# First block of a sliding-window attention: far scores preset in PSUM, two value products ahead, output weights split later, second norm's rows loaded sooner, the inverse roots of two tiles computed together

## The chip, the cores and the metric

The kernel runs on one core of a Trainium2 chip. The metric is the device time of one execution in microseconds; the median of three runs of the kernel before is 2051.01 (2048.93 to 2053.45).

## What is computed

Two layers of the same pair of blocks act on x, 2048 rows of 640 numbers. Each block normalizes its rows first and adds its result to x.

```
def _A_ref(x, dft_seq_re, dft_seq_im, dft_hid_re, dft_hid_im):
    a = jnp.einsum("bsd,ed->bse", x, dft_hid_re)
    b = jnp.einsum("bsd,ed->bse", x, dft_hid_im)
    y = jnp.einsum("ts,bse->bte", dft_seq_re, a) - jnp.einsum("ts,bse->bte", dft_seq_im, b)
    return y
...
    H = 32; Dh = D // H; W = 256
    ...
    scores = jnp.einsum("bhqd,bhkd->bhqk", q, k) * (Dh ** -0.5)
    idx = jnp.arange(S)
    mask = (idx[:, None] - idx[None, :] >= 0) & (idx[:, None] - idx[None, :] < W)
    scores = jnp.where(mask[None, None], scores, -1e9)
    p = _softmax(scores, axis=-1)
    o = jnp.einsum("bhqk,bhkd->bhqd", p, v)
    return (lambda x, *d: x.transpose(*d))(o, 0, 2, 1, 3).reshape(B, S, D) @ wo
...
x = x + _A_ref(_layernorm(x, axis=-1), ...)
x = x + _B_ref(_layernorm(x, axis=-1), B_wqkv, B_wo)
x = x + _A_ref(_layernorm(x, axis=-1), ...)
x = x + _B_ref(_layernorm(x, axis=-1), B_wqkv, B_wo)
```

The layer norm is (x - mean) / sqrt(variance + 1e-5), without weights. A query sees its own key and the 255 before it.

## The kernel before

The program is four stages, one after the other: `spectral(0)`, `attention(0)`, `spectral(1)`, `attention(1)`. In the profiled execution attention 0 runs from about 553 to 1062 us and attention 1 from about 1565 to 2052 us.

**Steps of an attention.** The 2048 rows are 16 tiles of 128 (index `i`), two of which make a block of 256 rows (`b`, 0 to 7). The main loop counts steps `G`; a block has 16 of them, and each step takes two of the 16 pairs of heads of one tile. In the code `g` is 2 G and `r` its place in a block of 32. One step issues, in this order:

- `scores`: TensorE computes the scores of this step's heads against the tile two back ("far", a = 0) into the front of the PSUM tiles `sk` (called `farq`), and against the tile before and its own tile (a = 1, 2) into the PSUM tiles `sq` (`near`). There is one `sq` and one `sk` for each of two partition groups `pi`, and no second buffer: the scores of the next step wait until this step's are read.
- `by_key`: the transposed scores of the step 8 before, into the rest of `sk`.
- `largest`, once for each `pi`: VectorE copies by a mask (L1175, COPY_PREDICATED) those far scores that a query sees into `near`, over those of its own tile that it doesn't see, and takes the largest of each query (L1177, TENSOR_REDUCE into `m`). In the first block (`i` < 2, steps 0 to 15) no far tile exists; then the copy reads `neg`, a 128 x 128 tile in SBUF filled with -1e20, broadcast over the two heads.
- after odd steps `part_tops` on GpSimd (POOL), `hand_on` of the maxima, `probabilities` (a sigmoid on ScalarE, L1231, and one or two affine selects on POOL, L1235 and L1237), `values` of step G - 11, and `back` (RECIPROCAL `r` and TENSOR_TENSOR `o` on VectorE, L1279 and L1280, then POOL's two ops on `os`).
- one *unit* of 15 matmuls (`run_unit`): a part of the projections to queries and keys (`proj_qk`), to values (`proj_v`), of the output product (`out_tile`, whose sum with x on VectorE is L956), or of the next stage.
- `slow_step`: one `yield` of the slow work in the queues `slow` and `idle`. It may not be issued ahead of the step's last reduction (`tc.issue_after(topped[0])`). How often it is called is in `STEPS`: once in even steps, twice in odd ones, and once more in the first steps (g below 14).

**Slow work.** `rows_norm` normalizes two tiles of x for the block after next: `norm_steps` (statistics on VectorE, an inverse square root by three Newton steps, L148 to L152, and the scaled rows `lny`, L166), then `split` into two fp16 parts, for which POOL does a subtraction into `rx` (L178). In the root, every op works on one column of 128 numbers, for the two tiles one after the other: two ops, then three times L151 and L152. Its x rows (`x2`) are loaded by SP's DMA queue some steps ahead, at most one pair at a time. `split_wo` splits the output weights into fp16 parts `bo` (ScalarE L1013, VectorE L1014); in layer 0 it is put into `idle` ahead of the main loop. `next_norm` does one tile's norm for the next spectral stage.

**Ahead of the loop**, `run_fill(FIRST_FILL)` issues units of the first value product until 2000 ns are spent: one of 15 matmuls (15 x 136 ns).

`marks` and `in_line` keep the order of instructions on one engine as written: an instruction issued within `in_line("dve")` is placed no sooner than the last one marked "dve". Otherwise the tile scheduler places the instructions of each engine.

Of the kernel before, what the change touches and what calls it, by code (L numbers as in the profile page):

```python
# [11 lines left out]
F32 = mybir.dt.float32  # L12
# [22 lines left out]
THIN_TO = (240, 264)  # L35
FIRST_FILL = 2000
FILL_LAST = 8
# [8 lines left out]
BACK_LAG = 12  # L46
STEPS = ((1, 2), (1, 2))
MUST_TO = 20
# [24 lines left out]
def body(ctx: ExitStack, tc: tile.TileContext, x_in, cmat, whid, wqkv, wo, out):  # L73
# [14 lines left out]
    mask = pers.tile([P, P], I32, name="mask")  # L88
    neg = pers.tile([P, P], F32, name="neg")
    shift = pers.tile([P, 1], F32, name="shift")  # L90
# [3 lines left out]
    def constants():  # L94
        make_identity(nc, idf[:])
        nc.vector.tensor_copy(idh, idf)
        nc.gpsimd.memset(mask, 1)
        nc.gpsimd.memset(neg, NEG)
        nc.gpsimd.memset(shift, SHIFT)
        for k in range(2):  # L100
            nc.gpsimd.memset(ones[:, k], M_UP if k else 0.0)
            nc.sync.dma_start(ones_d[k].rearrange("a (b c) -> (a b) c", c=2 * NP * QB // P), ones[:, k])
        nc.gpsimd.affine_select(out=mask, in_=mask, pattern=[[1, P]], base=0, channel_multiplier=-1,
                                compare_op=OP.is_gt, fill=0.0)
# [27 lines left out]
    def norm_steps(xs, ys, act=False):  # L132
# [12 lines left out]
        ts = nc.vector.tensor_scalar  # L145
        for k in range(n):
            h, g, u = (t[:, m, k:k + 1] for m in range(3))
            ts(h, mv[:, k, 1:2], 1e-5, -0.5 * X_UP ** -2, op0=OP.add, op1=OP.mult)  # L148
            ts(g.bitcast(I32), h.bitcast(I32), -0.5, ROOT, op0=OP.mult, op1=OP.add)
            for m in range(3):  # L150
                ts(u, g, g, h, op0=OP.mult, op1=OP.mult)  # L151
                normed[0] = ts(g, u, 1.5, g, op0=OP.add, op1=OP.mult).ins  # L152
                if m == 0:
                    yield
            if act:
                normed[0] = ts(u, mv[:, k, 0:1], g, -1.0, op0=OP.mult, op1=OP.mult).ins
            yield
# [688 lines left out]
    def attention(layer, proj, dst, final):  # L846
        with ExitStack() as st:
# [11 lines left out]
            farq = [t[:, :2 * P].rearrange("p (e c) -> p e c", e=2) for t in kst]  # L859
            tps = [t[:, 2 * P:].rearrange("p (a e c) -> p e a c", a=3, e=2) for t in kst]  # L860
            in_turn[0] = True
            VS_ = {}
# [80 lines left out]
            def out_tile(i):  # L943
                ot = OT[i]
                x3 = x2 = X2.pop(i)
                for n in range(2):
# [3 lines left out]
                    for dt in range(ND):  # L950
                        for l, r in ((0, 0), (0, 1), (1, 0)):
                            matmul(pf[:, :320], ot[:, l, dt], bo[r][:, dt, cs], start=k == 0, stop=k == 14)
                            k += 1
                            if k < 15:
                                yield 136
                    nc.vector.scalar_tensor_tensor(x3[:, cs], pf[:, :320], beta, x2[:, cs], op0=OP.mult, op1=OP.add)  # L956
                    yield 136
# [210 lines left out]
            def largest(G, pi):  # L1168
                i, p0 = place(2 * G)
                n, k = divmod(G, 2)  # L1170
                if k == 0 and pi == 0:
                    TOP[n] = sb.tile([P, 2, 2, 2], F32, tag="m", name="m", bufs=3)
                far = farq[pi] if i >= 2 else neg[:, None, :].to_broadcast([P, 2, P])
                with in_line("dve"):
                    marks["dve"] = nc.vector.copy_predicated(near[pi][:, :, 0], mask[:, None, :].to_broadcast([P, 2, P]), far).ins  # L1175
                with in_line("dve"):
                    marks["dve"] = nc.vector.tensor_reduce(TOP[n][:, pi, :, k], near[pi][:, :, :1 + (i >= 1)], axis=AX.XY, op=OP.max).ins  # L1177
                topped[0] = marks["dve"]
# [138 lines left out]
            def slow_step():  # L1317
                with tc.issue_after(topped[0]), in_line("act"):
                    for line in (slow, idle):
# [9 lines left out]
            spent[0] = credit[0] = 0.0  # L1329
            if layer == 0:  # L1330
                idle.append(split_wo())
            def due(G, lag):
                n, m = divmod(G - lag, 2)
                return n if m == 0 and 0 <= n < NG // 4 else None

            wanted, x2s, normed_at = [], [], [-FREE_STEPS]
            turned_back = []
            for G in range(NS // 2 + 1):
# [36 lines left out]
                if g < NG and c < NBQ and (g == 0 or r == X2_STEP):  # L1375
                    wanted.append(c)
                if wanted and x2s and g >= x2s[0] + 4 * (g > 0):
                    slow.append(rows_norm(wanted.pop(0), x2s.pop()))
                    x2s.clear()
                if slow:  # L1380
                    normed_at[0] = g
                if wanted and not slow and not x2s and g >= normed_at[0] + FREE_STEPS:
                    x2s += [g, [keep.tile([P, D], F32, tag="res0", name="x2", bufs=2) for t in range(2)]]
                    for t in range(2):
                        load(x2s[1][t], x2_d[2 * wanted[0] + t])
                if g < NG and r == ROWS_STEP:
                    flush(("v", b))
# [4 lines left out]
                if g < NG and r == HIDDEN_STEP:  # L1392
                    if b == NBQ - 1 and not final:
# [3 lines left out]
                        for k in range(2):  # L1397
                            fill.append(Unit(g + NEXT_STEPS[k], hidden.stage(k, None, once=True), "next", NG + k))
                for _ in range(STEPS[layer][G % 2] + (g < ROWS_STEP)):
                    slow_step()  # L1400
# [18 lines left out]
                if ran and turned_back:  # L1419
                    with in_line("dve"):  # L1420
                        back(turned_back.pop())
            while unit[0] is not None or fill or slow or idle or later:
                now[0] += 1
# [38 lines left out]
```

## Time and profile before

| | us |
|---|---|
| median of three runs | 2051.01 |
| profiled execution | 2055.41 |
| its span | 2053.7 |
| around the span | 1.7 |
| TensorE (PE) busy | 1986.1 |
| VectorE (DVE) busy | 1568.6 |
| GpSimd (POOL) busy | 1475.1 |
| ScalarE (ACT) busy | 1112.4 |

The profile is one execution; its times are microseconds from the span's start. A row of the timeline gives start, duration, engine, line and operation, the tile written and those read, and in brackets the idle time of the engine before it with what ended it. `xN` is a count of instructions. `pf<-big,early` is a product of values or of the output, `pf<-early,big` of queries and keys. The row of a window gives its length, then the busy time of PE, of its weight loads, of DVE, ACT and POOL, and then the granted clock of TensorE as a share of the full one.

### The profile page before, as it was taken

How to read it: one execution, taken by the hardware profiler on the slowest of the kernel's cores; microseconds unless marked ns; L12 is line 12 of the kernel's file. 1: busy time of each engine (PE TensorE's matmuls, PEld its weight loads, DVE VectorE, ACT ScalarE, POOL GpSimd, SP SyncE). 2: the span in 40 equal slices, each digit the busy share in tenths (PEclk: the TensorE clock that was granted, in tenths of full speed). 3: DMA queues.
4: the chain of work that ended last, by engine and by line, in shares of the span. 5: the costliest groups of instructions: out<-in, count | busy, mean ns of one | idle time of the engine just before them, and what ended most of it. 6: DMA issues, size and time to landing. Idle time of an engine off the chain costs nothing.

```text
span 2053.7 us, 55762 instructions
## 1 busy us (share of the span) xinstructions
PE 1986.1 (97%) x21881; PEld 1449.5 (71%) x21881; DVE 1568.6 (76%) x3261; ACT 1112.4 (54%) x1959; POOL 1475.1 (72%) x2168
## 2 busy tenths in 40 slices
PE   6999999999989999999999999999999999999998
PEld 4777777776767777777667777777676677777765
DVE  8888778768588888777648778787776788886673
ACT  5544555534247777666644444444332576766665
POOL 5777788877457788776657778777783587777754
PEclk9999999999999999999999999999999999999999
DMA  7556566566544544434645455454744454443232
GB/s 274 178 197 203 174 209 226 179 242 215 148 111 102 126 125 112 105 93 103 166 132 177 153 184 178 151 172 145 284 161 129 88 129 118 120 121 95 72 85 74
DMA packets 280508, 311.10 MB, mean 151 GB/s; under 512 B 107572, under 2 KB 214836, under 8 KB 271156
## 3 DMA queue, kind: packets, MB, share of 16 engines
q1 hardware_dynamic: 279668, 306.88, 50.0%
q8 instruction: 171, 2.80, 0.6%
q14 instruction: 93, 0.76, 0.1%
q10 hardware_dynamic: 576, 0.66, 0.1%
HBM read 201.72 MB, written 83.46 MB: 139 GB/s over the span
## 4 chain that ended last, share of the span: by engine, by line
PE 69%; DVE 14%; issue 5%; POOL 4%; DMA 4%; ACT 3%; SPq 0%; DVEq 0%; POOLq 0%; ACTq 0%
PE pf L126 32%; PE y L126 11%; PE x L126 11%; PE z L126 7%; PE sk L126 5%; DVE cc L558 3%; PE sq L126 3%; DVE sq L1175 2%; DVE m L1177 2%; ACT ptq L1231 2%; DMA res<-accd 2%; DVE lnt L151 1%; POOL cs L548 1%; DVE res L581 1%; DVE lnst L139 1%
## 5 line engine op out<-in xcount | busy, mean ns | idle before, releaser
L126 PEld LDWEIGHTS <-cc 128*128 128x128 f16 x5376 | 524.4, 98 | 213.1 <-issue 13.4
L1231 ACT ACTIVATE ptq<-sk,shift,alpha 128x768 f32<-128x768 f32 (+2 forms) x512 | 472.5, 945 | 122.9 <-PE sk L126 70.7
L126 PEld LDWEIGHTS <-big 128*128 128x128 f16 x4320 | 415.1, 99 | 131.0 <-issue 25.0
L1177 DVE TENSOR_REDUCE m<-sq 128x2 f32<-128x512 f32 (+1 forms) x512 | 345.6, 675 | 19.4 <-POOL os L1282 0.5
L126 PE MATMUL pf<-early,big 128*128 128x256 f16 x2400 | 295.1, 277 | 0.1
L555 ACT ACTIVATE cc<-cs 128x512 f16<-128x512 f32 x256 | 153.7, 625 | 260.3 <-POOL cs L548 149.8
L126 PE MATMUL y<-zc,cc 128*128 128x320 f16 x1728 | 262.8, 299 | 3.2 <-DVE pf L581 3.2
L1235 POOL TENSOR_SCALAR_AFFINE_SELECT ptq<-ptq 128x512 f32<-128x512 f32 x224 | 142.7, 637 | 167.7 <-ACT ptq L1231 165.1
L558 DVE SCALAR_TENSOR_TENSOR cc<-cs,cc 128x512 f16<-128x512 f32 x256 | 248.1, 978 | 7.6 <-ACT cc L555 7.5
L1175 DVE COPY_PREDICATED sq<-mask,sk 128x256 f32<-128x256 int32 x448 | 189.5, 423 | 53.4 <-PE sq L126 51.6
L558 DVE SCALAR_TENSOR_TENSOR cc<-cq,cc 128x512 f16<-128x512 f32 x192 | 205.8, 1073 | 0.1
L126 PE MATMUL pf<-ptq,v 128*32 128x128 f32 (+1 forms) x3840 | 183.6, 329 | 3.1 <-DVE x L956 2.6
L126 PE MATMUL z<-zc,cc 128*128 128x320 f16 x1152 | 177.7, 299 | 5.4 <-DVE res L581 4.4
L1237 POOL TENSOR_SCALAR_AFFINE_SELECT ptq<-ptq 128x512 f32<-128x512 f32 x256 | 166.1, 649 | 19.6 <-ACT ptq L1231 19.4
L126 PE MATMUL x<-zc,cc 128*128 128x320 f16 x1152 | 177.7, 299 | 0.0
L387 ACT ACTIVATE qf<-pf 128x256 f32<-128x256 f32 x160 | 61.2, 383 | 166.1 <-PE pf L126 132.8
L126 PEld LDWEIGHTS pf<-ptq,v 128*32 128x32 f32 x3840 | 110.7, 110 | 45.5 <-DVE x L956 3.9
L126 PE MATMUL pf<-big,early 128*128 128x320 f16 x960 | 141.4, 300 | 0.0
L547 POOL TENSOR_TENSOR cs<-cq 128x512 f32<-128x512 f32 x64 | 86.8, 1357 | 68.3 <-DVE cc L558 67.7
L126 PEld LDWEIGHTS <-qs 62*128 62x128 f16 x2688 | 90.3, 94 | 59.1 <-issue 55.8
L126 PE MATMUL pf<-bo,ot 128*128 128x320 f16 x840 | 123.8, 300 | 0.8 <-DVE x L956 0.8
L126 PE MATMUL x<-big 128*128 128x320 f16 x825 | 122.3, 299 | 2.0 <-DVE big L447 2.0
(144 smaller groups left out, 3484.3 us busy)
## 6 DMA issues: line engine op xcount, KB each, us to landing
cq<-in_cmat_dram SPq DMA_DIRECT2D x64, 1024.0 KB
accd<-res SPq DMA_DIRECT2D x96, 320.0 KB
res<-accd SPq DMA_DIRECT2D x96, 320.0 KB
x<-x2d SPq DMA_DIRECT2D x64, 320.0 KB
qkd<-early SPq DMA_DIRECT2D x160, 128.0 KB
ks<-qkd SPq DMA_DIRECT2D x108, 160.0 KB
qs<-qkd SPq DMA_DIRECT2D x84, 160.0 KB
x2d<-res SPq DMA_DIRECT2D x32, 320.0 KB
```

The costliest lines, as they stand in the source:

```text
L126: i = getattr(nc.tensor, what)(*args, **kw)
L139: nc.vector.bn_stats(st[:, h], x[:, h * 320:(h + 1) * 320])
L151: ts(u, g, g, h, op0=OP.mult, op1=OP.mult)
L387: nc.scalar.activation(f, pf[:, :QB], AF.Copy, scale=down)
L547: g.tensor_tensor(s1, a21, a22, op=OP.add)
L555: nc.scalar.activation(cc[m][:, 0], f, AF.Copy, scale=C_UP)
L558: nc.vector.scalar_tensor_tensor(cc[m][:, 1], f, C_UP, cc[m][:, 0], op0=OP.mult, op1=OP.subtract)
L1175: marks["dve"] = nc.vector.copy_predicated(near[pi][:, :, 0], mask[:, None, :].to_broadcast([P, 2, P]), far).ins
L1177: marks["dve"] = nc.vector.tensor_reduce(TOP[n][:, pi, :, k], near[pi][:, :, :1 + (i >= 1)], axis=AX.XY, op=OP.max).ins
L1231: marks["act"] = nc.scalar.activation(o[:, pi], tps[pi][:, :, first:], AF.Sigmoid, bias=shift, scale=alpha[:, 0:1]).ins
L1235: nc.gpsimd.affine_select(out=q[:, :, a0], in_=q[:, :, a0], pattern=[[0, 4], [-1, P]], base=0, channel_multiplier=1, compare_op=OP.is_gt, ...
L1237: ins = nc.gpsimd.affine_select(out=q[:, :, a0 + 2], in_=q[:, :, a0 + 2], pattern=[[0, 4], [1, P]], base=0, channel_multiplier=-1, compare ...
```

## The change

1. `FIRST_FILL` is 4000: two units of the first value product are issued ahead of the loop.
2. The front of both `sk` tiles is set to -1e20 by VectorE at the start of each attention, and the masked copy reads it there in the first block too. `neg` and POOL's memset of it are gone.
3. `split_wo` goes into `idle` at g = 14 and not ahead of the loop.
4. The times at which a pair's rows are loaded and its norm may begin are set otherwise: a load may be issued as soon as the norm before has ended, and the norm itself keeps the distance.
5. `norm_steps` for more than one tile works on both columns at once: two TENSOR_SCALAR, then three times two TENSOR_TENSOR and a SCALAR_TENSOR_TENSOR.
6. In even steps the slow steps are issued behind the unit, and slow work is placed no sooner than the last sum of an output tile (`marks["x"]`).

```
-FIRST_FILL = 2000
+FIRST_FILL = 4000
...
-STEPS = ((1, 2), (1, 2))
+STEPS = (1, 2)
...
-        for k in range(n):
+        if n > 1 and not act:
+            h, g, u = (t[:, m] for m in range(3))
+            ts(h, mv[:, :, 1], 1e-5, -0.5 * X_UP ** -2, op0=OP.add, op1=OP.mult)
+            ts(g.bitcast(I32), h.bitcast(I32), -0.5, ROOT, op0=OP.mult, op1=OP.add)
+            for m in range(3):
+                nc.vector.tensor_tensor(u, g, g, op=OP.mult)
+                nc.vector.tensor_tensor(u, u, h, op=OP.mult)
+                normed[0] = nc.vector.scalar_tensor_tensor(g, u, 1.5, g, op0=OP.add, op1=OP.mult).ins
+                yield
+        for k in range(n if n == 1 or act else 0):
...
+            for f in farq:
+                nc.vector.memset(f, NEG)
...
-                    nc.vector.scalar_tensor_tensor(x3[:, cs], pf[:, :320], beta, x2[:, cs], op0=OP.mult, op1=OP.add)
+                    marks["x"] = nc.vector.scalar_tensor_tensor(x3[:, cs], pf[:, :320], beta, x2[:, cs], op0=OP.mult, op1=OP.add).ins
...
-                far = farq[pi] if i >= 2 else neg[:, None, :].to_broadcast([P, 2, P])
...
-                    marks["dve"] = nc.vector.copy_predicated(near[pi][:, :, 0], mask[:, None, :].to_broadcast([P, 2, P]), far).ins
+                    marks["dve"] = nc.vector.copy_predicated(near[pi][:, :, 0], mask[:, None, :].to_broadcast([P, 2, P]), farq[pi]).ins
...
-                with tc.issue_after(topped[0]), in_line("act"):
+                with tc.issue_after(topped[0]), in_line("act"), in_line("x"):
...
-            if layer == 0:
-                idle.append(split_wo())
...
-            wanted, x2s, normed_at = [], [], [-FREE_STEPS]
+            wanted, x2s, normed_at = [], [], [-2 * FREE_STEPS]
...
-                if wanted and x2s and g >= x2s[0] + 4 * (g > 0):
+                if wanted and x2s and g >= max(x2s[0] + 4 * (g > 0), normed_at[0] + 2 * FREE_STEPS):
...
-                if wanted and not slow and not x2s and g >= normed_at[0] + FREE_STEPS:
+                if wanted and not slow and not x2s and g > normed_at[0]:
...
+                if layer == 0 and g == ROWS_STEP:
+                    idle.append(split_wo())
...
-                for _ in range(STEPS[layer][G % 2] + (g < ROWS_STEP)):
+                steps = STEPS[G % 2] + (g < ROWS_STEP)
+                for _ in range(steps if G % 2 else 0):
...
+                for _ in range(0 if G % 2 else steps):
+                    slow_step()
```

What stands on VectorE shows it best. These rows are VectorE's order before, in the first block of attention 0, from the second reduction of step 0 to the second copy of step 2 (`sq` of one number is group 0, of the other group 1):

```order
L1177 TENSOR_REDUCE m<-sq_6969 128x2
L1175 COPY_PREDICATED sq_6968<-mask,neg 128x256
L1177 TENSOR_REDUCE m<-sq_6968 128x2
L1175 COPY_PREDICATED sq_6969<-mask,neg 128x256
L1177 TENSOR_REDUCE m<-sq_6969 128x2
L1014 SCALAR_TENSOR_TENSOR bo_67<-wst,wsc,bo_66 128x640
L1175 COPY_PREDICATED sq_6968<-mask,neg 128x256
L1014 SCALAR_TENSOR_TENSOR bo_67<-wst,wsc,bo_66 128x640
L1177 TENSOR_REDUCE m<-sq_6968 128x2
L1175 COPY_PREDICATED sq_6969<-mask,neg 128x256
```

And these are the same place in the changed kernel, whose line numbers are some higher (the masked copy is L1183, the reduction L1185), from the two new memsets on:

```order
L869 MEMSET sk_6963 128x256
L869 MEMSET sk_6964 128x256
L1183 COPY_PREDICATED sq_6961<-mask,sk_6963 128x256
L1185 TENSOR_REDUCE m<-sq_6961 128x2
L1183 COPY_PREDICATED sq_6962<-mask,sk_6964 128x256
L1185 TENSOR_REDUCE m<-sq_6962 128x2
L1183 COPY_PREDICATED sq_6961<-mask,sk_6963 128x256
L1185 TENSOR_REDUCE m<-sq_6961 128x2
L1183 COPY_PREDICATED sq_6962<-mask,sk_6964 128x256
L1185 TENSOR_REDUCE m<-sq_6962 128x2
```

The two ops on `bo` have left this place (they stand behind the reductions of step 11 now), and every copy reads `sk` in place of `neg`.

The second place is the root of a pair in a later block, as it stands in VectorE's order before, from the last reduction of step 43 to the first copy of step 44:

```order
L1177 TENSOR_REDUCE m<-sq_6969 128x2
L148 TENSOR_SCALAR lnt<-lnmv 128x1
L149 TENSOR_SCALAR lnt<-lnt 128x1
L151 TENSOR_SCALAR lnt<-lnt 128x1
L152 TENSOR_SCALAR lnt<-lnt 128x1
L151 TENSOR_SCALAR lnt<-lnt 128x1
L152 TENSOR_SCALAR lnt<-lnt 128x1
L151 TENSOR_SCALAR lnt<-lnt 128x1
L1279 RECIPROCAL r<-pf 128x8
L152 TENSOR_SCALAR lnt<-lnt 128x1
L1280 TENSOR_TENSOR o<-pf,r 128x160
L1175 COPY_PREDICATED sq_6968<-mask,sk_6970 128x256
```

The changed kernel has there:

```order
L1185 TENSOR_REDUCE m<-sq_6962 128x2
L146 TENSOR_SCALAR lnt<-lnmv 128x2
L147 TENSOR_SCALAR lnt<-lnt 128x2
L149 TENSOR_TENSOR lnt<-lnt 128x2
L150 TENSOR_TENSOR lnt<-lnt 128x2
L151 SCALAR_TENSOR_TENSOR lnt<-lnt 128x2
L149 TENSOR_TENSOR lnt<-lnt 128x2
L150 TENSOR_TENSOR lnt<-lnt 128x2
L151 SCALAR_TENSOR_TENSOR lnt<-lnt 128x2
L1287 RECIPROCAL r<-pf 128x8
L1288 TENSOR_TENSOR o<-pf,r 128x160
L1183 COPY_PREDICATED sq_6961<-mask,sk_6963 128x256
```

Eight ops of one column, which are all of the first tile's root, became eight of two columns, which are two thirds of both tiles' roots; both `r` and `o` stand behind them. The rest of the root and the second tile's, four steps of slow work before, shrink to three ops behind the reductions of step 44.

On TensorE the matmuls are the same; a unit of the value product (15 x `pf<-big,early`) stands ahead of the first scores of each attention now, and the units of the following steps move up. The transposes of the first norms in `spectral(0)` stand two matmuls later.

More of the change, by code (lines that the diff above doesn't have):

```diff
@@ L88, in body @@
     mask = pers.tile([P, P], I32, name="mask")
-    neg = pers.tile([P, P], F32, name="neg")
     shift = pers.tile([P, 1], F32, name="shift")
@@ L97, in constants @@
         nc.gpsimd.memset(mask, 1)
-        nc.gpsimd.memset(neg, NEG)
         nc.gpsimd.memset(shift, SHIFT)
```

## The prediction

> **What bounds the kernel now.** I read the page first (busy shares), then the windows around the first block of each attention, then PE's waits there and its timeline, and last VectorE (DVE) and GpSimd (POOL) side by side.
>
> ```profile
> span 2053.7 us, 55762 instructions
> PE 1986.1 (97%) x21881; PEld 1449.5 (71%) x21881; DVE 1568.6 (76%) x3261; ACT 1112.4 (54%) x1959; POOL 1475.1 (72%) x2168
> ```
>
> TensorE is the bound: only 2053.7 - 1986.1 = 67.6 us of the span are without a matmul. A change that leaves the matmuls as they are can win only from those gaps and from stretches where the matmuls run at a lower clock. The windows show both; PEclk is the granted TensorE clock, and PE's busy time stands right behind the length of the window.
>
> ```profile
> 575.00:590.00 15.00, 12.47 (x106) 9.56 (x106) 10.74 (x25) 4.42 (x11) 9.61 (x18) 0.89 0.46 101
> 590.00:625.00 35.00, 32.82 (x381) 22.45 (x381) 30.21 (x76) 20.08 (x43) 20.59 (x45) 0.95 0.46 101
> ...
> 1585.00:1600.00 15.00, 12.47 (x96) 9.12 (x95) 9.49 (x19) 4.35 (x10) 10.00 (x18) 0.77 0.51 116
> 1600.00:1632.00 32.00, 29.65 (x346) 20.33 (x344) 26.25 (x69) 17.11 (x37) 17.05 (x38) 0.95 0.45 90
> ```
>
> In these four windows, the first blocks of the two attentions, PE idles 2.53, 2.18, 2.53 and 2.35 us, and the missing clock is 15 x 0.11 = 1.65, 35 x 0.05 = 1.75, 15 x 0.23 = 3.45 and 32 x 0.05 = 1.60 us. Together 9.6 us of idling and 8.45 us of clock. PE's waits say what ends the idling. The first two rows are the window 556 to 575, the next is 575 to 700, then 1585 to 1700, and the last one 700 to 960.
>
> ```profile
> PE sq L126 <- DMA x2d<-res: 2.1, 1, 2.1
> PE sq L126 <- DVE m L1177: 2.0, 3, 1.2
> ...
> PE sq L126 <- DVE m L1177: 5.0, 7, 1.5
> ...
> PE sq L126 <- DVE m L1177: 4.7, 6, 1.5
> ...
> PE pf L126 <- DVE x L956: 2.1, 5, 0.8
> ```
>
> PE's timeline shows the places (start, duration, in brackets the idle time before):
>
> ```profile
> 557.44 0.27 PE L126 MATMUL sq<-ks 62*128 62x128 f16 x3 [2.11 <-DMA x2d<-res]
> 557.64 2.21 PE L126 MATMUL pf<-big,early 128*128 128x320 f16 x15
> ...
> 568.42 3.45 PE L126 MATMUL pf<-early,big 128*128 128x256 f16 x30
> ...
> 581.99 0.21 PE L126 MATMUL sq<-ks 62*128 62x128 f16 x1 [1.53 <-DVE m L1177]
> 583.20 0.38 PE L126 MATMUL sq<-ks 62*128 62x128 f16 x7 [1.00 <-DVE m L1177]
> ...
> 583.67 5.12 PE L126 MATMUL pf<-early,big 128*128 128x256 f16 x30
> ...
> 609.82 0.21 PE L126 MATMUL sq<-ks 62*128 62x128 f16 x1 [1.05 <-DVE m L1177]
> 610.77 0.38 PE L126 MATMUL sq<-ks 62*128 62x128 f16 x7 [0.74 <-DVE m L1177]
> ```
>
> A score tile `sq` exists once per partition group, so the scores of step G+1 wait for both reductions of step G on DVE. Where DVE is late, PE stands, and right behind the stall of 1.53 + 1.00 us the same 30 matmuls that took 3.45 us take 5.12: the stall is paid a second time, in clock. A stall of 1.05 + 0.74 us is followed by the 0.95 of its window, while the one gap of 2.11 us at 557 is not (the 30 behind it take 3.45 us). So some 1.8 to 2.5 us idle, spread over a few us, seems to be where the clock goes. The Trainium skill (TensorE: Matmul & The Clock Gate, "HAM oscillation") puts the point at idle gaps over some 3.4 us. These rows differ, since no gap here is over 2.2 us; by the page the clock would be no part of the gain, and the 7.2 us worked out below would be 2 x (2.53 - 1.5) = 2.1.
>
> **The change part by part.** *Two value products ahead.* PE gets 15 matmuls more, 2.21 us by the row at 557.64, ahead of the first scores; they are moved, not added. They cover the 2.11 us in which the first scores of layer 0 wait for the stack's DMA: 2.0 gone. Layer 1 has no such wait. The products are missing later, so that other units move up; nothing hides less by it, since every step still gets a unit while any is left.
>
> *Output weights split later.* In layer 0 two of these ops sit among the first steps' reductions:
>
> ```profile
> 564.25 0.88 DVE L1014 SCALAR_TENSOR_TENSOR bo<-wst,wsc,bo 128x640 f16<-128x640 f32 x1 [1.81 <-ACT bo L1013]
> ...
> 565.89 0.88 DVE L1014 SCALAR_TENSOR_TENSOR bo<-wst,wsc,bo 128x640 f16<-128x640 f32 x1 [0.41 <-ACT bo L1013]
> ```
>
> Without their 2 x 0.88 us and the 0.41 us of waiting for ScalarE, of the 2.0 us of waiting for `m` in this stretch 0.2 stay: 1.8 gone. They come back as a pair behind step 11, where DVE also has the second norm's statistics: there they cost between nothing and 1.76 us. I take 1.5, since PE waits for DVE in that stretch already.
>
> *Far scores preset.* The masked copy of the first 16 steps reads `neg` from SBUF, that of all later ones `sk` from PSUM:
>
> ```profile
> L1175 DVE COPY_PREDICATED sq<-mask,sk 128x256 f32<-128x256 int32 x448 | 189.5, 423 | 53.4 <-PE sq L126 51.6
> ...
> L1175 DVE COPY_PREDICATED sq<-mask,neg 128x256 f32<-128x256 int32 x64 | 33.9, 529 | 21.2 <-PE sq L126 21.2
> ```
>
> 64 x (529 - 423) ns = 6.8 us of DVE time disappear, and not evenly: they are in few copies, beside POOL's work. First DVE, then POOL:
>
> ```profile
> 579.78 1.63 DVE L1175 COPY_PREDICATED sq<-mask,neg 128x256 f32<-128x256 int32 x1
> ...
> 579.45 1.67 POOL L178 TENSOR_TENSOR rx<-lny,rx 128x640 f16<-128x640 f32 x1
> ```
>
> The copy ends 0.29 us after POOL's op, as if it had started when that ended. This 1.63 in place of 0.42 is most of the 1.53 us stall at 581.99. With the far operand in PSUM there is one SBUF input left, and the 448 copies with `sk` show no such stretch in their mean. The two memsets a layer are between nothing and 2 x 0.42 us; DVE has nothing else while PE waits for the stack or finishes the products, so nothing.
>
> Around steps 4 to 8 that makes: now 2.53 + 1.65 = 4.2 us in layer 0 and 2.53 + 3.45 = 6.0 us in layer 1. The copies give back 1.2 + 0.4 us each time and the shorter root some 1; I leave 1.5 us a layer for what stays, the two wide `lny` ops and the root's ops among the reductions. Gain 2.7 + 4.5 = 7.2 (between 4, if the clock still falls, and 10.2).
>
> *Second norm's rows sooner, roots as one.* The root of two tiles is now 16 ops of one column, interleaved:
>
> ```profile
> L151 DVE TENSOR_SCALAR lnt<-lnt 128x1 f32<-128x1 f32 x192 | 50.8, 269 | 4.1
> L152 DVE TENSOR_SCALAR lnt<-lnt 128x1 f32<-128x1 f32 x192 | 39.6, 211 | 4.0
> L149 DVE TENSOR_SCALAR lnt<-lnt 128x1 int32<-128x1 int32 x64 | 9.3, 145 | 1.4
> L148 DVE TENSOR_SCALAR lnt<-lnmv 128x1 f32<-128x1 f32 x64 | 9.1, 142 | 0.2
> ```
>
> Per pair 6 x 0.269 + 6 x 0.211 + 2 x 0.145 + 2 x 0.142 = 3.45 us. After: 11 ops on two columns, nine of them with two SBUF inputs; at about 0.15 us each (a row below has that for a one-column op of two inputs) some 1.7 us. In the stretch of the second norm (590 to 625, 1600 to 1632) idling and clock are 3.9 us in either layer. Less root, no held copies, the loads of its rows sooner: 2.0 a layer, less the 1.5 for the output weights in layer 0. Gain 2.5 (0 to 5).
>
> *Slow steps behind the unit, and behind `x`.* PE waits 2.1 us for `x` in layer 0, where a wide op stands ahead of it:
>
> ```profile
> 737.31 0.70 DVE L166 TENSOR_SCALAR lny<-x,lnmv,lnt 128x640 f32<-128x640 f32 x1
> ```
>
> The output tile's sum goes first now; 1.3 of the 2.1 go, and about as much as one of 0.8 in layer 1: gain 2.1.
>
> *First spectral stage.* Its norms of tile pairs use the joint root too; PE waits 1.47 us for a tile there:
>
> ```profile
> 35.63 0.45 PE L126 MATMUL pf<-idh,xs 128*128 128x128 f16 x5 [1.47 <-POOL xs L178]
> ```
>
> A chain shorter by up to 1.7 us may take that away or be hidden by the DMA-fed start: 0 to 1.5, I take 0.5.
>
> *What the joint root can cost.* In the later blocks a pair's root stands after an odd step's reductions, ahead of `r`, `o` and the next copy (43rd step; first DVE, then POOL, then PE):
>
> ```profile
> 711.49 0.14 DVE L148 TENSOR_SCALAR lnt<-lnmv 128x1 f32<-128x1 f32 x1
> ...
> 713.71 0.42 DVE L1175 COPY_PREDICATED sq<-mask,sk 128x256 f32<-128x256 int32 x1
> ...
> 715.23 0.69 DVE L1177 TENSOR_REDUCE m<-sq 128x2 f32<-128x512 f32 x1
> ...
> 711.75 0.64 POOL L1237 TENSOR_SCALAR_AFFINE_SELECT ptq<-ptq 128x512 f32<-128x512 f32 x1
> ...
> 713.56 0.68 POOL L389 TENSOR_TENSOR early<-qf,early 128x256 f16<-128x256 f32 x1
> ...
> 715.98 0.22 PE L126 MATMUL sq<-ks,qs 62*128 62x128 f16 x2
> ```
>
> The last reduction ends at 715.92, the matmul that needs it starts at 715.98: no slack. Now the root's one-column ops run at their usual length beside a busy POOL. The new ones have two inputs, and small two-column ops have been held:
>
> ```profile
> 222.82 0.75 DVE L716 TENSOR_SCALAR wexp<-wexp 128x2 int32<-128x2 int32 x1
> ...
> 222.68 0.86 POOL L611 TENSOR_TENSOR res<-res,pf 128x320 f32<-128x320 f32 x1
> ...
> 223.95 0.15 DVE L719 TENSOR_TENSOR alpha<-wexp 128x1 f32<-128x1 f32 x1
> ```
>
> If each of the six two-input ops lets one POOL op past, they follow POOL's ops from the end of the select at 712.39 to that of the product at 714.24, and with their own 0.3 us and the 0.5 of `r` and `o` the copy starts near 715.05 instead of 713.71: 1.35 us, all on the path. If none is held, the copy starts a little sooner, which wins nothing. There are four such pairs a layer, eight in all: 0 to 8 x 1.35 = 10.8, and 12 with the tail of each root in the next step. POOL is not as full at each, so I take 0.75 each: a loss of 6.
>
> **Sum.** 2.0 + 1.8 + 7.2 + 2.5 + 2.1 + 0.5 = 16.1 gained, 6 lost: 10 us off the profiled execution, 2053.7 + 1.7 around the span = 2055.4, so 2045.4. The median of the runs is 2051.0; 10 off is 2041.0.
>
> **Rivals.** *The small ops are not held* (20%). Then the loss is nothing to 1.5 and the gain stays 16: 2035.0. For it: one-column ops between POOL's never stretch. Against: the 0.75 us row.
>
> *Every two-input op is held behind POOL, and this decides* (10%, slower). The eight roots cost 1.5 each, 12 us; in the first blocks the roots' ops take the place of the held copies, the stalls stay above the 1.8 us at which the clock falls, and the 9.7 us of the two block-0 terms shrink to nothing. Left are 2.0 + 1.8 + 2.1 = 5.9: slower by 6, 2057.0. It decides from 1.5 us a root together with a block 0 that still stalls 1.8 us in one go. The Trainium skill has this rule (SBUF — State Buffer, "SBUF: two separate sides"): whichever starts first of a DVE op with two SBUF inputs and a GpSimd op holds the shared port for its whole length, and the other blocks. The copy at 579.78 agrees; no run shows it yet for ops of 0.15 us that come one behind the other.
>
> *The gain is mostly eaten* (20%): roots held at 1.35, clock still falling in one of the four windows; 16 - 11 - 2 = 3 off: 2048.0.
>
> **How the numbers follow.** The forecast has 50%, with its own range 2036.0 to 2046.0 from the terms' bounds. A run of this kernel can tell 0.2%, 4.1 us, from no change. Faster by more: the forecast's and the first rival's cases without their tails, 0.68; within: the eaten case and the rest of it, 0.21; slower 0.11. The range leaves out one in ten at either end: 2031.0 to 2050.0.
>
> **What would show it.** Right, if in the profile after the gap at 557 is gone, the copies with `sk` have 0.42 us from the first step on, the four windows have PEclk near 1.00, and only the eight places like 713 show a new wait of PE for `m`. Wrong, if root ops on two columns take 0.15 us everywhere (then faster), or if PEclk stays at 0.8 to 0.9 around 580 and 1590 with the roots stretched there (then slower).

## The result, and the profile after

The changed kernel takes 2056.44 us (median of 8 runs, 2053.79 to 2058.38), the kernel before 2051.51 in the same runs (8, 2048.24 to 2053.45): 1.0025 times as long, 95% interval 1.0016 to 1.0035. It is slower by 4.9 us; the forecast was 10 us faster.

The page of the changed kernel has PE at work for less time in a longer span. PE's 1986.1 - 1983.7 = 2.4 us less for the same matmuls fits a clock that was won back (granted 0.998 on the mean, 0.996 before), and the time without a matmul rose from 67.6 to 73.0 us.

```profile
span 2056.7 us, 55736 instructions
## 1 busy us (share of the span) xinstructions
PE 1983.7 (96%) x21881; PEld 1448.2 (70%) x21881; DVE 1558.8 (76%) x3200; ACT 1109.9 (54%) x1959; POOL 1467.0 (71%) x2167
```

The windows around the first blocks (length, PE's busy time and so on, as before) have full clock at 575 and 1585, but PE idles more in the second and the fourth, 6.18 and 3.51 us for 2.18 and 2.35:

```profile
575.00:590.00 15.00, 13.64 (x141) 10.34 (x139) 13.11 (x34) 6.59 (x15) 11.52 (x23) 1.00 0.50 127
590.00:625.00 35.00, 28.82 (x341) 20.12 (x340) 25.85 (x65) 19.20 (x40) 17.70 (x40) 0.95 0.56 114
1585.00:1600.00 15.00, 14.16 (x139) 11.03 (x138) 13.66 (x36) 4.35 (x11) 9.93 (x19) 1.00 0.30 74
1600.00:1632.00 32.00, 28.49 (x349) 20.15 (x346) 25.18 (x65) 18.79 (x40) 18.16 (x44) 1.00 0.56 119
```

PE's waits in the first block of attention 0 (555 to 640) and, behind the dots, of attention 1 (1565 to 1632) say why. What waited for `m` before, 7.0 and 4.7 us in these stretches, is down to 1.1 and 0.8, and a wait stands there that before did not have:

```profile
PE pf L124 <- DMA early<-rx: 5.2, 1, 5.2
PE sq L124 <- DVE m L1185: 1.1, 4, 0.6
...
PE pf L124 <- DMA early<-rx: 2.4, 1, 2.4
PE sq L124 <- DVE m L1185: 0.8, 2, 0.6
```

`early<-rx` is the transposing DMA of the normalized rows for the block after next; the query and key products of that block wait for it (PE's timeline):

```profile
594.19 0.85 PE L124 MATMUL pf<-ptq,v 128*32 128x256 f32 x16
600.27 3.07 PE L124 MATMUL pf<-early,big 128*128 128x256 f16 x15 [5.24 <-DMA early<-rx]
```

The 15 matmuls behind it take 3.07 us where 1.81 is usual: the clock falls here once more. SP's queue shows what stands ahead of the two DMAs now:

```profile
587.03 0.89 SPq L195 DMA_DIRECT2D wst<-in_wo_dram  x2
...
589.35 0.88 SPq L195 DMA_DIRECT2D x<-x2d  x2
590.28 7.86 SPq L203 DMA_TRANSPOSE early<-rx  x2
```

Before, SP had the first of them at 585.79, taking 2.23 us, ahead of the loads of x rows and of one of the weights' loads, and the second at 594.04 behind them:

```profile
585.79 2.23 SPq L196 DMA_TRANSPOSE early<-rx  x1
...
592.66 0.85 SPq L188 DMA_DIRECT2D x<-x2d  x2
593.56 0.42 SPq L188 DMA_DIRECT2D wst<-in_wo_dram  x1
594.04 2.07 SPq L196 DMA_TRANSPOSE early<-rx  x1
```

The rest of the loss stands in the later blocks. There the joint root is no shorter than the columns were, and its copy comes later. The 59th step, first DVE, then POOL, then ACT, then PE:

```profile
771.24 0.63 DVE L146 TENSOR_SCALAR lnt<-lnmv 128x2 f32<-128x2 f32 x1
771.91 0.17 DVE L147 TENSOR_SCALAR lnt<-lnt 128x2 int32<-128x2 int32 x1
772.11 0.16 DVE L149 TENSOR_TENSOR lnt<-lnt 128x2 f32<-128x2 f32 x1
...
773.21 0.52 DVE L151 SCALAR_TENSOR_TENSOR lnt<-lnt 128x2 f32<-128x2 f32 x1
...
774.19 0.42 DVE L1183 COPY_PREDICATED sq<-mask,sk 128x256 f32<-128x256 int32 x1
...
771.22 0.63 POOL L1245 TENSOR_SCALAR_AFFINE_SELECT ptq<-ptq 128x512 f32<-128x512 f32 x1
...
773.04 0.67 POOL L396 TENSOR_TENSOR early<-qf,early 128x256 f16<-128x256 f32 x1
...
774.65 0.99 ACT L1239 ACTIVATE ptq<-sk,shift,alpha 128x768 f32<-128x768 f32 x1 [0.88 <-DVE sq L1183]
...
775.69 0.31 PE L124 MATMUL sk<-ks,qs 62*128 62x128 f16 x4 [0.64 <-ACT ptq L1239]
```

The two-column TENSOR_SCALAR takes 0.63 us, to the end of POOL's select, and the last op of the step 0.52, to that of POOL's product; those between take 0.16. From the root's first op to the copy it is 774.19 - 771.24 = 2.95 us, where the same root took 2.26 before. At all eight later roots this stretch is longer, 2.66 to 2.96 us for 2.22 to 2.26, 4.5 us together. The second sigmoid starts behind the copy, and PE waits for the sigmoid.

A table says where the 3.0 us between the two spans are. A column is what a stage added to the shift of the same matmuls against the profile of before; each row is one execution. The changed kernel's row adds up to 2.3 us, and its other 0.7 come behind the last matmul:

| kernel | spectral 0 | block 0 of attention 0 | later blocks, to 960 | 960 to 1050 | spectral 1 | block 0 of attention 1 | later blocks, to 1960 |
|---|---|---|---|---|---|---|---|
| changed | +4.6 | -4.8 | +3.4 | +1.6 | +0.7 | -5.3 | +2.1 |
| x2_behind | +2.3 | -8.9 | +3.4 | 0.0 | +1.0 | -6.6 | +2.0 |
| wo_later | +2.1 | -7.8 | +2.8 | 0.0 | -0.7 | -5.4 | +2.1 |
| both_behind | +2.2 | -10.3 | +2.8 | +1.6 | +1.0 | -6.1 | +2.1 |
| root_apart | +1.0 | -5.5 | -0.7 | 0.0 | -0.4 | -5.3 | -1.0 |
| b_root | +1.2 | -8.5 | +2.5 | +1.6 | +0.2 | -6.6 | +1.7 |
| b_farq | +1.4 | -9.4 | 0.0 | 0.0 | +0.5 | -7.2 | -0.1 |
| b_fill | -0.3 | -6.7 | 0.0 | 0.0 | +0.6 | -2.7 | 0.0 |
| best | +0.5 | -8.8 | -0.4 | +1.6 | +0.5 | -7.0 | -0.9 |
| farq_fill | +1.7 | -7.8 | -0.1 | +1.6 | +0.6 | -5.7 | 0.0 |
| farq_x | +0.7 | -8.0 | -0.1 | +1.6 | +1.0 | -5.7 | -0.1 |
| farq_fill_slow | +0.9 | -7.8 | -0.6 | +1.7 | +0.4 | -7.0 | -0.9 |
| a_neg | +2.0 | -2.6 | +3.9 | 0.0 | +0.7 | -3.8 | +2.1 |

It has to be read with one thing in mind: the profile of before lost much to the clock. It has five stretches of half clock of 3.4 us each in the first blocks, 8.5 us of loss; `b_fill`, which stalls near 582 and 1590 too, for 1.47 + 0.59 us, has one. And its 2055.41 us stands 5 to 7 us above the medians of 2048.7 to 2050.2 that the same kernel had beside the experiments. So the columns of the first blocks flatter every kernel, by some 3 us each if the two share this alike, and only differences between the other rows, and the medians, bear weight. The 1.6 at 960 to 1050 is one such stretch of half clock, which about half of the profiles have.

### The profile page after: what moved, and what is told of

Its sections match the earlier page's. It is cut to its first block, busy times and chain, and to the rows that moved or that the text cites. A ratio compares the mean times of both kernels' runs of the same rounds, so it can differ in the third digit from the quotient of the medians.

```text
span 2056.7 us, 55736 instructions
## 1 busy us (share of the span) xinstructions
PE 1983.7 (96%) x21881; PEld 1448.2 (70%) x21881; DVE 1558.8 (76%) x3200; ACT 1109.9 (54%) x1959; POOL 1467.0 (71%) x2167
## 4 chain that ended last, share of the span: by engine, by line
PE 68%; DVE 14%; issue 5%; ACT 5%; DMA 4%; POOL 3%; SPq 1%; DVEq 0%; ACTq 0%; POOLq 0%
PE pf L124 30%; PE y L124 11%; PE x L124 11%; PE z L124 8%; PE sk L124 5%; DVE cc L565 4%; PE sq L124 3%; ACT ptq L1239 2%; DVE sq L1183 2%; DVE m L1185 2%; DMA res<-accd 1%; DVE res L588 1%; DVE lnst L137 1%; DMA early<-rx 1%; SPq L195 1%
## 5 line engine op out<-in xcount | busy, mean ns | idle before, releaser
L1185 DVE TENSOR_REDUCE m<-sq 128x2 f32<-128x512 f32 (+1 forms) x512 | 345.3, 674 | 19.0
L124 PE MATMUL pf<-early,big 128*128 128x256 f16 x2400 | 289.7, 274 | 7.9 <-DMA early<-rx 7.7
L1183 DVE COPY_PREDICATED sq<-mask,sk 128x256 f32<-128x256 int32 x512 | 216.6, 423 | 74.2 <-PE sq L124 71.2
```

Source lines behind the costliest of these rows:

```text
L124: i = getattr(nc.tensor, what)(*args, **kw)
```

## The experiments

Times are medians of the runs of each kernel, beside the kernel before on the same chip (ratio with its 95% interval).

**Loads of the second norm's rows behind the transposing DMAs** (x2_behind).

```
-                if wanted and not slow and not x2s and g > normed_at[0]:
-                    x2s += [g, [keep.tile([P, D], F32, tag="res0", name="x2", bufs=2) for t in range(2)]]
-                    for t in range(2):
-                        load(x2s[1][t], x2_d[2 * wanted[0] + t])
...
                 run_later()
+                if wanted and not slow and not x2s and g > normed_at[0]:
+                    x2s += [g, [keep.tile([P, D], F32, tag="res0", name="x2", bufs=2) for t in range(2)]]
+                    for t in range(2):
+                        load(x2s[1][t], x2_d[2 * wanted[0] + t])
```

> The changed kernel, with the loads of the second norm's rows issued behind the two transposing DMAs of the first norm's rows in the same step, not ahead of them. Theory Q (SP's queue): the new stalls of PE for the transposed rows (5.24 us in attention 0, 2.42 in attention 1) come from the loads that the change put ahead of these DMAs. Then attention 1's stall is at most 0.3 us, attention 0's falls to about 2.5 (the output weights' loads are still ahead), and the time is 4.5 to 6.5 us below the changed kernel's 2056.4: about 2051. Rival V (products): PE comes too early, since one value product more was spent ahead of the loop, and the rows could not be there anyway: both stalls stay within 1 us, time 2055.5 to 2057.

Measured: 2048.82 us, 0.9984 (0.9975 to 0.9992) of before; 7.6 us below the changed kernel. The stalls fell to 2.39 and 1.10 us:

```profile
595.16 1.80 PE L124 MATMUL pf<-early,big 128*128 128x256 f16 x15 [2.39 <-ACT bo L1022]
```

The first is of the size that theory Q has, though what came last there is ScalarE's op on `bo` and not the DMA, so that not all of it need be the queue's. The second is not as in Q: 1.1 us stays with no load of rows ahead.

**Output weights' loads behind them** (wo_later).

```
-                if layer == 0 and g == ROWS_STEP:
+                if layer == 0 and g == ROWS_STEP + 4:
```

> The changed kernel, with the output weights' split put into its queue two steps later (g = 18, not 14), so that its first loads stand behind the transposing DMAs. Theory Q: attention 0's stall of 5.24 us falls to about 2.4, what attention 1 has, which keeps its 2.42; the clock's loss of 1.7 us behind the stall may go with it; time 2052 to 2054. Rival V: no change, 2055.5 to 2057.

Measured: 2052.44 us, 1.0011 (1.0001 to 1.0020). The stall in attention 0 is 2.46 us, that of attention 1 stays with 2.35:

```profile
594.98 1.80 PE L124 MATMUL pf<-early,big 128*128 128x256 f16 x15 [2.46 <-DMA early<-rx]
```

Moving either pair of loads, 2 x 320 KB, takes 2.8 us off the 5.24.

**Both** (both_behind), the two edits together.

> The changed kernel with both: the second norm's loads and the output weights' loads behind the transposing DMAs. Theory Q: both stalls at most 0.3 us, each transposing DMA 1.3 to 1.6 us of SP's time and not 2.0 to 3.9; 5.24 + 2.42 + 1.7 of clock less: about 2047. Rival V: stalls stay, 2055 to 2057.

Measured: 2048.84 us, 0.9990 (0.9980 to 1.0000). SP's two DMAs take 3.43 us together in attention 0, in place of 7.86:

```profile
586.40 3.43 SPq L203 DMA_TRANSPOSE early<-rx  x2
589.93 1.53 SPq L195 DMA_DIRECT2D x<-x2d  x2
...
593.18 0.88 SPq L195 DMA_DIRECT2D wst<-in_wo_dram  x2
```

Of the 5.24 us stall of the changed kernel 0.68 are left in `both_behind`, now put down to ScalarE; in attention 1 1.63 of 2.42 stay. So theory Q holds for attention 0, but for the last 0.68. For attention 1 it explains a third to a half; there PE is sooner than the rows, as rival V has it, but by the joint root and not by the product (see `root_apart`). No more was gained in the time than with the first edit alone; a wait of 1.19 us for another DMA (`ks<-htd`) stands behind the stall now.

**The root column by column again** (root_apart).

```
-        if n > 1 and not act:
+        if False:
-        for k in range(n if n == 1 or act else 0):
+        for k in range(n):
```

> The changed kernel with the inverse root column by column again, all else as changed. Theory L (held roots): the eight later roots each cost some 0.5 us on the path (the stretch 640 to 965 is 3.3 us longer than before, 1630 to 1965 2.1), so these stretches fall back to what they were before within 1 us. The first spectral stage, 4.6 us longer than before, falls back by 3 or more if the joint root there (its start has other idle times) set it off, and stays if not. The stalls of the first blocks change their place, since the root has more steps again and the second tile's rows come later; so 2046 to 2053 in all. Rival: the roots are not it, and 640 to 965 stays 2 or more longer than before.

Measured: 2043.41 us, 0.9961 (0.9949 to 0.9973); 13 us below the changed kernel, and below the 2046 to 2053 expected. The later blocks fell back from +3.4 to -0.7 and from +2.1 to -1.0, so the joint root cost 4.1 + 3.1 = 7.2 us there, as theory L has it. The wait for the transposed rows is gone too, with all four loads still ahead of the first DMA and the two products still ahead of the loop. With more steps in the root the second tile's rows, and the units that need them, are later in the plan. The product that waits in the changed kernel is the same one in every kernel; here is where PE runs it in the kernel before, in root_apart and in b_root (the next experiment):

```profile
604.35 1.80 PE L126 MATMUL pf<-early,big 128*128 128x256 f16 x15
...
602.90 2.75 PE L124 MATMUL pf<-early,big 128*128 128x256 f16 x15
...
592.71 1.80 PE L126 MATMUL pf<-early,big 128*128 128x256 f16 x15
```

PE comes to it at 600.27 - 5.24 = 595.03 in the changed kernel. In every kernel with the joint root in the first block it stands behind 96 matmuls of scores of its attention, in every other behind 120, two steps of scores more, whatever the number of products ahead of the loop. So it is the joint root that brings PE to the rows sooner, and the 5.24 us take both, the loads ahead and the joint root: b_root, with the joint root and one load ahead, doesn't wait there. In its place are stalls of 1.74 us for `m` at 580 and 1586 (with an `lny` of 1.38 us, of which below) and one of 2.43 at 600, where the copy stands behind the two ops on `bo` (1.91 us together) and a norm's statistics.

**The joint root alone, on the kernel before** (b_root): the new branch of `norm_steps` and nothing else.

> The kernel before with the joint root alone (all norms of two tiles, the first spectral stage's too). Theory L: alone it costs in the later blocks what the changed kernel shows there, 3 to 3.5 us in 640 to 965 and 2 to 3 in 1632 to 1960, and about 1 in the first spectral stage; what it gives in the first blocks (a shorter chain ahead of two stalls) is 0 to 4: slower than before by 2 to 7 us. Rival: as short ops it is no worse than the columns; within 2 us of before.

Measured: 2049.08 us, 0.9995 (0.9986 to 1.0003): the same. The loss in the later blocks came, at +2.5 and +1.7 somewhat below what was expected, but the first blocks gave it back. The forecast of 2 to 7 slower was too high. The waits for `m` in the first blocks, 7.0 and 4.7 us before, fall to 3.0 and 1.1 although the copies still read `neg`:

```profile
PE sq L126 <- DVE m L1186: 3.0, 6, 0.8
...
PE sq L126 <- DVE m L1186: 1.1, 4, 0.6
```

So the preset is not the only edit that ends these stalls.

**The preset far scores alone, on the kernel before** (b_farq).

```
+            for f in farq:
+                nc.vector.memset(f, NEG)
...
-                far = farq[pi] if i >= 2 else neg[:, None, :].to_broadcast([P, 2, P])
```

> The kernel before with the far scores preset alone. Theory F (held copies): the copies of the first 16 steps all take 0.42 to 0.45 us, the two pairs of stalls at 582 and 1590 (1.53 + 1.00 us) lose 1.2 to 2 us each, the clock behind at least one of them stays full, and the time falls by 4 to 8 us. Rival: the stalls come from the root's and the wide ops' length, a pair loses less than 0.5 us, and the time stays within 2 us.

Measured: 2040.58 us, 0.9957 (0.9944 to 0.9970): 9 us faster, by itself, than before. All 512 copies take the same time now:

```profile
L1174 DVE COPY_PREDICATED sq<-mask,sk 128x256 f32<-128x256 int32 x512 | 216.5, 423 | 67.8 <-PE sq L124 65.2 <-PE pf L124 0.9
```

Of the waits for `m` in the two first blocks, 7.0 and 4.7 us before, 1.6 and 0.5 are left (555 to 640, then 1560 to 1632), and no stretch of half clock stands in either. A wait for another DMA, `ks<-htd`, which before did not have, takes 1.2 and 1.5 us of it:

```profile
PE sq L124 <- DVE m L1176: 1.6, 6, 0.6
PE sk L124 <- DMA ks<-htd: 1.2, 1, 1.2
...
PE sk L124 <- DMA ks<-htd: 1.5, 1, 1.5
PE sq L124 <- DVE m L1176: 0.5, 2, 0.3
```

**Two value products ahead alone, on the kernel before** (b_fill): `FIRST_FILL = 4000`.

> The kernel before with two value products ahead, alone. Theory: attention 0's wait of 2.11 us for the stack goes, nothing else of size; 1 to 2.5 us faster. Rival V: the product is missing later, PE comes to the units that need the second block's rows sooner, and a new wait for the transposed rows of 1 us or more stands at 595 to 605 or 1605 to 1612; then no gain.

Measured: 2047.27 us, 0.9984 (0.9974 to 0.9993): 3.3 us faster. No new wait stands at 600, so rival V fell. The stalls for `m` are those of before in attention 1 (4.5 us for 4.7) and somewhat less in attention 0 (4.8 for 7.0). The wait for the stack is gone. But that is no proof for the edit: `b_farq` and `b_root`, which issue one product ahead as before, don't have that wait either. Here is where `b_farq`'s first scores run, without idle time before them:

```profile
556.49 0.29 PE L124 MATMUL sq<-ks 62*128 62x128 f16 x4
```

So the 2.11 us may have belonged to the one execution that was profiled.

**The two together** (farq_fill).

> The kernel before with the preset far scores and two value products ahead. Theory A (the two add up): the 2.11 us at the start of attention 0, which the preset alone no longer has in its profile, is hidden for good, and the unit that comes sooner costs nothing: 0 to 3 us below the preset alone (2040.6): 2038 to 2041. Rival V (the product is missing later): a wait of 1 us or more for the transposed rows near 590 to 600, since PE runs some 10 us sooner there than before: 2041 to 2044.

Measured: 2043.28 us, 0.9976 (0.9965 to 0.9986), which is not below the preset alone. Both of my theories fell, though the time lies within the second's range: there is no wait for rows, and the gains don't add up. A new stall stands at 582 (1588 in attention 1):

```profile
582.03 0.38 PE L124 MATMUL sq<-ks 62*128 62x128 f16 x7 [1.75 <-DVE m L1176]
582.34 0.22 PE L124 MATMUL pf<-idh,tops 128*16 128x128 f16 x1
582.50 3.12 PE L124 MATMUL pf<-early,big 128*128 128x256 f16 x15
```

DVE's timeline has the cause ahead of it, and POOL's beside it: the second `lny` starts behind POOL's subtraction into `rx` and ends with it, after 1.38 us.

```profile
579.81 1.38 DVE L164 TENSOR_SCALAR lny<-x,lnmv,lnt 128x640 f32<-128x640 f32 x1
...
579.44 1.40 POOL L176 TENSOR_TENSOR rx<-lny,rx 128x640 f16<-128x640 f32 x1 [0.20 <-ACT rx L175]
```

With the preset alone the same op comes ahead of POOL's and takes 0.61 us, and POOL's starts as it ends:

```profile
576.77 0.61 DVE L164 TENSOR_SCALAR lny<-x,lnmv,lnt 128x640 f32<-128x640 f32 x1
...
577.41 1.40 POOL L176 TENSOR_TENSOR rx<-lny,rx 128x640 f16<-128x640 f32 x1
```

So with the product ahead, the only difference between the two kernels, the order in which the two start is another; that it comes by the units of the next steps, which move, was not followed up.

**Slow work behind the last sum with x** (farq_x): farq_fill and the mark `x`.

> As farq_fill, and slow work no sooner than the last sum of an output tile (the mark x), without moving the even steps' slow work behind the unit. Theory: the waits of PE for x (0.53, 0.81 and 0.81 us before) go, and no wait for qf of 0.78 comes: 1 to 2.2 us below farq_fill. Rival: the mark alone moves nothing; within 0.7 us of farq_fill in the stretches 640 to 960 and 1632 to 1960.

Measured: 2041.63 us, 0.9968 (0.9955 to 0.9980). The time is 1.7 us below farq_fill's, where the theory had it, but the two kernels' single times overlap, and the profile speaks for the rival. The mark alone moves nothing: the waits for x stay (0.50 and 0.81 us), the later blocks are within 0.1 us.

**And the even steps' slow work behind the unit** (farq_fill_slow).

> As farq_x, and the even steps' slow work behind the unit. Theory: the three waits for x go, and the changed kernel's two waits of 0.78 us for qf in attention 0 come with it, because the wide fp16 split for the next stage stands ahead of qf on ScalarE: attention 0 gains and loses alike (within 0.7 us of farq_fill in 640 to 960), attention 1 gains 0.8. Rival: the waits for qf belong to the joint root's shorter chain and don't show here; then 2 us below farq_fill.

Measured: 2041.22 us, 0.9962 (0.9948 to 0.9976). The three waits for x go. In attention 0 two waits for ScalarE, of 0.77 and 0.42 us, take the place of most of them, so that its later blocks gain 0.6 us, those of attention 1 0.9, as the theory has it. The longer one:

```profile
685.65 2.20 PE L124 MATMUL pf<-bo,ot 128*128 128x320 f16 x15 [0.77 <-ACT qf L385]
```

**The changed kernel without the preset** (a_neg): `neg` and the `far` line put back.

> The changed kernel with the far operand of the first 16 steps read from neg in SBUF again. Theory F: the copies beside POOL's subtraction are held again, stalls of PE for m of 1.5 us or more stand near 582 and 1590, the clock falls there, and the time is 4 to 9 us above the changed kernel's 2056.4: 2060 to 2065; where it stalls sooner, the wait for the transposed rows shrinks by as much, so 2057 is the low end. Rival: the copies were not it, 2055 to 2057.

Measured: 2057.45 us, 1.0045 (1.0032 to 1.0057). What alone is worth 9 us is worth 1 to 4 here, by the medians or by the ratios; the time is at the low end that was named. The stall at 582 is back, PE comes to the products with the rows 36.2 us after its first scores and not 33.3, and its wait for the rows is shorter (3.36 us for 5.24):

```profile
582.56 0.38 PE L126 MATMUL sq<-ks 62*128 62x128 f16 x7 [1.60 <-DVE m L1186]
...
598.72 1.65 PE L126 MATMUL pf<-early,big 128*128 128x256 f16 x7 [3.36 <-DMA early<-rx]
```

**All that held** (best): both loads behind, the joint root only for an attention's first two norms.

```
-        if n > 1 and not act:
+        if joint:
...
+                yield from norm_steps(x2s, ys, joint=b <= 3)
```

> The changed kernel with the second norm's and the output weights' loads behind the transposing DMAs, and the joint root only in the first two norms of an attention; the later ones and the first spectral stage column by column. Theories Q and L together: first blocks as with both loads behind (10 and 6 us below before), later blocks as with the root apart (0.5 to 1 below before each), first spectral stage within 1 us of before: about 17 us below the profile of before, a time of 2036 to 2041. If the gains don't add up, 2042 to 2048.

Measured: 2039.58 us, 0.9949 (0.9936 to 0.9962): 17 us below the changed kernel, 10 below before. PE's waits for the sigmoid in its later blocks (640 to 965) are 0.6 us where `both_behind` has 3.0 (2.0 in the changed kernel):

```profile
PE sk L124 <- ACT ptq L1239: 0.6, 2, 0.4
...
PE sk L124 <- ACT ptq L1239: 3.0, 6, 0.6
```

It beats both kernels, and so does the preset alone, which is within 1 us of it, too close to tell them apart, and is one edit.

## Why the prediction was wrong

**The step that failed: "Less root, no held copies, the loads of its rows sooner: 2.0 a layer."** It counted as gains two things that together made a new wait, and didn't ask what the loads are queued ahead of. In SP's queue they, and the output weights' loads that were moved with no price for their DMAs, came ahead of the first norm's transposing DMAs. These took 7.86 us and not the 2.23 + 2.07 = 4.30 of before. The shorter root, for its part, brought the products that read these rows two steps forward. PE waited 5.24 and 2.42 us, and it lost the clock behind the first. Put behind, the loads bring 7.6 us back, and so do the x rows' loads alone. Without the joint root there is no such wait even with the loads ahead (root_apart).

The plan keeps the distance for such a DMA in steps (`TURN_LAG`, six of `g`, which are three steps), so where PE stalls less, that distance is shorter in microseconds: in a_neg, where the stall for `m` at 582 is back, the wait for the rows is 3.36 us for 5.24. That "nothing hides less by it", of the products ahead, has no run against it; of their gain, the 2.0 us for the stack are in doubt, as said above.

**The preset: right in kind, and more than I took.** The first blocks' stalls by held copies were forecast at 7.2 us; alone the preset is worth 9. In the changed kernel the stalls for `m` went as forecast (from 7.0 and 4.7 us to 1.1 and 0.8), and the rows' wait ate it. But a held copy is not the only way to such a stall: in farq_fill, with the preset, 1.75 us stand at 582 behind a held `lny`, and in b_root, without it, the long stalls are gone. Which op starts beside POOL's subtraction decides, and any edit that shifts the order changes that.

**The clock: priced as if it were certain.** The 8.45 us of half clock in the profile of before were one execution's. With stalls near 582 and 1590 as before, `b_fill` lost one stretch where before lost five. In farq_x a stall of 1.75 us at 582 costs no clock, and one of 1.74 at 1587 costs a stretch of 3.41 us at half clock, 1.7 us.

**The joint root: right size, other mechanism.** Forecast 6 us in the later blocks, measured 7.2, 0.9 a root. The two-input ops were mostly not held: in the later roots they slip in between POOL's short ops at 0.16 us, but for one or two of six. Held were the two-column TENSOR_SCALAR ops, which I took for free: 0.80 to 0.88 us for the two, where the one-column pair took some 0.29. The stretch from the root to the copy has 4.5 of the 7.2 us; where the other 2.7 are was not followed up. The wait is PE's for the sigmoid, which waits for the copy, and not for `m`. Held against the rule of the Trainium skill that was the slower rival (SBUF — State Buffer, "SBUF: two separate sides"), the rows show both: who starts behind a POOL op is held to its end, and an op of 0.16 us often finds POOL between two ops.

**Waits for x: forecast 2.1, got 0.6 and 0.9** in farq_fill_slow, without the joint root. Waits for ScalarE's copy of `qf` took their place in attention 0, 0.77 and 0.42 us there and 0.78 twice in the changed kernel; the longer one of farq_fill_slow stands behind the wide split for the next stage. I had named no work that the moved slow steps would be put ahead of.

**First spectral stage: forecast 0.5 less, got 4.6 more.** The other kernels with the joint root there have 1.2 to 2.3 more in their profiles, those without it -0.3 to 1.7; b_farq, which leaves that stage as it was, has 1.4. So about 1 us of it is the root's by the means of the two groups, 1.7 is a stretch of half clock at 36.3 that no other kernel has, and the cause of the remainder stays open; b_farq and b_fill, which both leave the stage alone, lie 1.7 apart.

**Output weights later:** the 1.8 us at 567 went, and at the new place the split cost 2.4 us and a stretch of half clock in root_apart, more than the 1.5 taken.

The rival on the other side, 2057.0 with a chance of one in ten, has the time, but by luck and not for its reason: the first blocks' stalls for `m` did go, and a root costs 0.9 us and not 1.5.

## What to carry to other kernels

When a load or its issue is moved, list what it passes in its queue, and what waits for that; the price is paid by the transfer behind it. In a plan that counts steps, a stall removed at one place makes every later distance shorter in time, so the next transfer on the list has to be checked before the gain is booked. The same holds for a shorter chain: it brings its reader forward too. A wait that one profile shows may belong to that execution; look for it in a second before it is priced. Of a change with many parts, measure each alone: here the preset alone gave as much as the best combination, the products ahead alone about 3 us and nothing on top of the preset, and the loads ahead and the later joint roots took 17 us away.

## What the runs showed of the hardware

A transposing DMA took 1.33 and 1.55 us of SP's queue in a late block of the kernel before (at 1877), 2.07 to 2.72 in its first blocks, and 3.90 each in the changed kernel behind four loads of 320 KB (7.86 us for two). A TENSOR_SCALAR on 128x2 fp32 can be held by POOL (0.63 us beside an op that ended then; the least in that kernel is 0.21); the 512 one-column ops of the roots in the kernel before took 0.09 to 0.28, none longer. And the order of start decides between DVE and POOL: the same `lny` took 0.61 us ahead of POOL's subtraction and 1.38 behind its start.
